# One batch row ahead of the other three: reordering a two-layer decode step so that w_up and w_down are read once

## Chip, cores, metric

The kernel runs on one core of a Trainium2 chip. The time is the device time of one execution in microseconds (us). Executions come in a fast and a slow state; the medians and ratios below are those of fast runs alone. PE is the matmul engine, DVE the vector engine, ACT the scalar engine, and SP the engine whose queue issues the loads. The recorded texts call a row a batch, the gated block glu and layer norm LN. A "tile" here is 1 MiB of the on-chip arena (128 partitions x 4096 bf16), and most loads fill one tile.

## The reference

Two identical layers, with the same weights and the same K and V caches, on four batch rows of one token each. Every layer is a windowed attention and a gated block, each with a residual:

```python
x = x + A(layernorm(x), k_cache, v_cache, wq, wo)   # 32 heads, 8 KV heads, window 2048, head size 128
x = x + B(layernorm(x), w_gate, w_up, w_down)       # sigmoid(x @ w_gate) * (x @ w_up) @ w_down, F = 1792
x = x + A(...)                                      # the same K, V and weights again
x = x + B(...)
```

In bf16 the used part of K is 16 MiB and of V 16 MiB, wq and wo are 4 MiB each, and w_gate, w_up and w_down are 1.75 MiB each. All of it is more than the arena holds (25 tiles), so part of it is read twice.

## The kernel before

It plans all work as operations with tokens that they read and write, orders them per engine with a simple list scheduler, and emits five in-order instruction streams. Loads go out from one queue in a fixed order, and a load can be issued only when a tile of a small pool is free. All 16 K tiles stay in the arena from layer 1 to layer 2; V is read twice (but for two tiles), wq twice, and the gated block's weights twice. A unit of attention is one KV head of all four batch rows: K transposes on DVE (layer 1 only), scores S on PE, softmax on DVE and ACT, a transpose of the probabilities on PE, then PV on PE, then wo.

```python
pool.free = list(range(4 * HKV, NS, 2))        # 9 tiles for all that is not K
# ... load order: what comes next is taken when a tile is free
load_wq(0)
# ... K and V of layer 1 by head, wo
load_glu(0)                                    # w_gate, w_up, w_down
load_wq(1)
# ... V of layer 2 in reverse order of heads, all but two tiles that were kept
load_glu(1)                                    # w_gate, w_up, w_down once more, last of all

def attn(L):                                   # 8 units, one KV head of 4 rows each
    # ...
    for ui, h in enumerate(hs):
        if ui + 2 < HKV:
            ks[ui + 2] = front(ui + 2)         # scores and softmax, two units ahead
        ov = pv_unit(tag, h, ks[ui], v_tiles[(L, h)])          # 2 tiles, 64 matmuls
        if ui + 2 < HKV:
            turn_p("%d.%d" % (L, ui + 2), ks[ui + 2])          # transposed probabilities
        wo_unit(tag, h, ov, ks[ui], ui == 0, ui == HKV - 1)    # 16 matmuls

# the program
q_proj(0, 0, NB)
attn(0)
glu(0, 0, NB)
layer_norm("Q", 0, NB)
q_proj(1, 0, NB)
attn(2)
glu(1, 0, NB, True)
```

## Time and profile before

| | before |
|---|---|
| median (2 runs) | 185.54 us (185.33 to 185.75) |
| span of the profiled run | 184.4 us |
| bytes on the load queue | 71.84 MB |
| mean DMA rate | 391 GB/s |
| busy share of PE, DVE, ACT | 55%, 49%, 19% |

From the page of the kernel before (busy time by engine; tenths of busy time in 40 equal slices; the load queue; the chain of waits that ended last):

```profile
span 184.4 us, 4421 instructions
PE 101.2 (55%) x1944; PEld 54.7 (30%) x1944; DVE 89.5 (49%) x221; ACT 35.7 (19%) x100; POOL 14.8 (8%) x77
...
DMA  5999999999999999999999999999999999999980
GB/s 198 425 427 427 425 403 391 411 421 419 409 387 425 419 421 403 392 419 419 400 391 414 412 407 393 403 350 417 330 396 419 419 423 416 418 416 402 412 341 24
...
q1 hardware_dynamic: 15352, 71.84, 97.2%
...
DMA 52%; PE 25%; SPq 16%; DVE 4%; issue 2%; ACT 0%
```

The DMA row is at 9 everywhere but at the two ends, and no compute engine is busy for 60% of the span. The kernel is bound by its stream of loads. The Trainium skill ("Perfetto Trace Analysis", Roofline) says that a single core is bounded by its 16 DMA engines at about 435 GB/s; this trace reaches 427.

The same by stage: most of layer 1's attention (0 to 83), the rest of it (to 107.4), the boundary between layers (to 129.1, where layer 2's first score matmul starts), layer 2's attention (to 171.5, the end of its last PV), and the tail. The columns are the stretch, its length, busy time with the number of instructions for each engine, granted PE clock, DMA share and GB/s:

```profile
0.00:83.00 83.00, 34.97 (x580) 16.11 (x580) 51.00 (x99) 15.31 (x42) 7.42 (x39) 0.75 1.00 401
83.00:107.40 24.40, 11.56 (x298) 8.76 (x298) 10.22 (x19) 1.91 (x4) 0.98 (x6) 0.50 1.02 407
107.40:129.10 21.70, 10.47 (x148) 4.33 (x148) 8.04 (x28) 2.42 (x10) 0.00 (x0) 0.50 1.01 393
129.10:171.50 42.40, 37.50 (x836) 22.10 (x832) 16.90 (x64) 14.58 (x39) 6.39 (x33) 0.82 1.01 405
171.50:184.40 12.90, 6.70 (x86) 3.36 (x86) 3.38 (x13) 1.52 (x6) 0.00 (x0) 0.74 0.62 248
```

The boundary is a serial chain of 21.7 us (PE busy for 10.5 of it), yet the stream runs through it at 393 GB/s, because there is always something left to read for later. And in layer 2's attention PE is busy for 37.5 of 42.4 us, so it is close behind the stream: eight units in 42.4 us are 5.3 us each (4.7 of them busy), while the two V tiles of a unit take 2 x 2.49 = 4.98 us to land.

### The profile page before, as it was taken

The page shows a single profiled execution, that of the slowest core. Times are in us where ns is not written, and L with a number is a line of the kernel's source. Part 1 is how long each engine was busy: PE and PEld are TensorE (multiplying, and loading weights), DVE is VectorE, ACT ScalarE, POOL GpSimd, SP SyncE. Part 2 cuts the span into 40 slices and gives each one's busy share as a digit, 9 for nine tenths or more (in the row PEclk, how much of TensorE's full clock was granted, in tenths as well). Part 3 has the DMA queues.
Part 4 walks back from the last instruction along what each step waited for, and adds up shares of the span by engine and source line. Part 5 has one row for each costly group of instructions (what it writes and reads, how often), then busy time and mean ns, then how long its engine had stood idle before and what let it go on. Part 6 is the DMA issues. An engine that isn't in the chain of part 4 may idle for free.

```text
span 184.4 us, 4421 instructions
## 1 busy us (share of the span) xinstructions
PE 101.2 (55%) x1944; PEld 54.7 (30%) x1944; DVE 89.5 (49%) x221; ACT 35.7 (19%) x100; POOL 14.8 (8%) x77
## 2 busy tenths in 40 slices
PE   0532423652807327173373545445979997994474
PEld 0101000332303323023232441210334653584422
DVE  5209998477592565925621531138463442340330
ACT  2003022240212103011020001001365442220010
POOL 4000000110000101010010000000022111120000
PEclk9999995585766756755555555555897897885569
DMA  5999999999999999999999999999999999999980
GB/s 198 425 427 427 425 403 391 411 421 419 409 387 425 419 421 403 392 419 419 400 391 414 412 407 393 403 350 417 330 396 419 419 423 416 418 416 402 412 341 24
DMA packets 15379, 72.12 MB, mean 391 GB/s; under 512 B 1144, under 2 KB 5248, under 8 KB 8704
## 3 DMA queue, kind: packets, MB, share of 16 engines
q1 hardware_dynamic: 15352, 71.84, 97.2%
q8 instruction: 15, 0.25, 0.5%
q14 instruction: 4, 0.03, 0.0%
q10 hardware_dynamic: 8, 0.00, 0.0%
HBM read 71.83 MB, written 0.00 MB: 390 GB/s over the span
## 4 chain that ended last, share of the span: by engine, by line
DMA 52%; PE 25%; SPq 16%; DVE 4%; issue 2%; ACT 0%
DMA arena<-in_A_v_cache_dram 33%; SPq L382 16%; PE ps L697 11%; DMA arena<-in_B_w_down_dram 9%; PE ps L770 8%; DMA arena<-in_A_wq_dram 5%; DMA arena<-in_B_w_up_dram 5%; PE ps L726 2%; PE ps L794 1%; DVE ps L492 1%; PE ps L626 1%; DVE nmax L705 1%; PE ps L749 1%; PE ps L905 1%; PE ps L852 1%
## 5 line engine op out<-in xcount | busy, mean ns | idle before, releaser
L770 PE MATMUL ps<-ebuf,arena 128*128 128x8 bf16 x1024 | 31.0, 167 | 29.7 <-DMA arena<-in_A_v_cache_dram 22.1
L697 PE MATMUL ps<-arena,qbd 128*16 128x512 bf16 x256 | 32.5, 626 | 16.9 <-DVE qbd L668 8.4
L770 PEld LDWEIGHTS ps<-ebuf,arena 128*128 128x128 bf16 x1024 | 28.8, 101 | 36.3 <-DMA arena<-in_A_v_cache_dram 32.5
L678 DVE STREAM_TRANSPOSE arena<-arena 128x1024 f32<-128x1024 f32 x32 | 37.9, 1219 | 3.3 <-DMA arena<-in_A_k_cache_dram 3.0
L705 DVE TENSOR_REDUCE nmax<-ps 128x1 f32<-128x512 f32 x16 | 11.0, 687 | 26.0 <-PE ps L697 26.0
L714 ACT ACTIVATE prow<-ps,nmax 128x512 bf16<-128x512 f32 x16 | 11.0, 687 | 39.6 <-DVE nmax L711 24.9
L671 ACT COPY qbd<-qrep 32x64 bf16<-32x64 bf16 x32 | 7.7, 241 | 40.9 <-PE ps L697 40.3
L697 PEld LDWEIGHTS ps<-arena,qbd 128*16 128x16 bf16 x256 | 6.1, 97 | 31.3 <-issue 22.0
L739 POOL CAST s<-psm 128x1 bf16<-128x1 f32 x16 | 3.0, 188 | 144.4 <-ACT prow L714 144.4
L778 DVE TENSOR_TENSOR onb<-ps,rinv 128x16 bf16<-128x16 f32 x16 | 2.9, 184 | 21.1 <-PE ps L770 21.1
L626 PE MATMUL ps<-arena,xn 128*4 128x512 bf16 x64 | 7.8, 582 | 7.6 <-DMA arena<-in_A_wq_dram 6.2
L794 PE MATMUL ps<-onb,arena 128*128 128x4 bf16 x256 | 9.1, 166 | 3.1 <-DVE onb L778 3.1
L731 ACT CAST prow<-ps 128x512 bf16<-128x512 f32 x16 | 9.4, 587 | 7.1 <-PE ps L726 7.0
L735 DVE STREAM_TRANSPOSE ebuf<-prow 128x256 f32<-128x256 f32 x16 | 7.0, 437 | 6.7 <-ACT prow L731 6.4
L852 PE MATMUL ps<-arena,xn 128*4 128x448 bf16 x64 | 6.5, 560 | 4.9 <-DVE xn L607 3.1
L794 PEld LDWEIGHTS ps<-onb,arena 128*128 128x128 bf16 x256 | 7.9, 101 | 4.1 <-DVE onb L778 2.8
L726 PE MATMUL ps<-prow,perm 64*128 64x256 bf16 x64 | 7.4, 315 | 2.4 <-ACT prow L714 2.3
L596 ACT ACTIVATE lnv<-lnv 128x4 f32<-128x4 f32 x4 | 0.8, 205 | 34.0 <-DVE lnv L593 34.0
L634 DVE STREAM_TRANSPOSE ebuf<-ps 128x512 f32<-128x512 f32 x4 | 2.9, 715 | 7.7 <-PE ps L626 7.6
L859 DVE STREAM_TRANSPOSE ebuf<-ps 128x448 f32<-128x448 f32 x4 | 2.6, 650 | 7.8 <-PE ps L852 7.8
L668 DVE COPY qbd<-qrep 32x64 bf16<-32x64 bf16 x32 | 5.3, 166 | 0.7 <-ACT qrep L657 0.2
L749 PE MATMUL ps<-sel_b,s 128*128 128x16 bf16 x48 | 3.8, 175 | 3.2 <-POOL s L743 2.4
(61 smaller groups left out, 68.1 us busy)
## 6 DMA issues: line engine op xcount, KB each, us to landing
arena<-in_A_v_cache_dram SPq DMA_DIRECT2D x30, 1024.0 KB, 16.8
arena<-in_A_k_cache_dram SPq DMA_DIRECT2D x16, 1024.0 KB, 16.0
arena<-in_A_wq_dram SPq DMA_DIRECT2D x8, 1024.0 KB, 9.4
arena<-in_A_wo_dram SPq DMA_DIRECT2D x4, 1024.0 KB, 24.3
arena<-in_B_w_gate_dram SPq DMA_DIRECT2D x4, 896.0 KB, 19.7
arena<-in_B_w_up_dram SPq DMA_DIRECT2D x4, 896.0 KB, 15.8
arena<-in_B_w_down_dram SPq DMA_DIRECT2D x2, 1024.0 KB, 12.5
arena<-in_B_w_down_dram SPq DMA_DIRECT2D x1, 768.0 KB, 7.0
```

What stands on the lines that cost most here:

```text
L382: o = P.op("sync", name, 0.0, lambda e, dst=dst, src=src: e.dma_start(dst, src), r=r, w=w, dma_bytes=nbytes, dma_rate=tm[rate])
L626: last = pe.matmul(ps[32 * hh:32 * hh + NB, qb, :], xn[:, c * NB:(c + 1) * NB], tile_ap(s)[:, o + hh * 512:o + (hh + 1) * 512], start=(c = ...
L671: P.op("scalar", "qe%s_%d" % (tag, a), c_act(64), lambda s_, dst=dst, src=src: s_.copy(dst, src), r=rd, w=[("q", k2, a)])
L678: P.op("vector", "T%d_%d" % (h, t), c_dve(1024), lambda v, v32=v32: v.transpose(v32, v32), r=[("slot", 4 * h + t)], w=[("slot", 4 * h + t)])
L697: last = pe.matmul(ps[32 * gi:32 * gi + NR, bank, :], qbd[:, q0:q0 + NR], kt[:, cp // 2, cp % 2, b % 2, :, :], start=(cp == 0), stop=(cp = ...
L705: lambda v: v.tensor_reduce(nmax[:, k2:k2 + 1], ps[:, bank, :], AXX, ALU.max),
L714: lambda a: a.activation(prow[:, :].rearrange("p (m x t) -> p m x t", x=16, t=2), ps[:, bank, :].rearrange("p (m t x) -> p m x t", x=16, t ...
L726: last = pe.matmul(ps[:, PBS[i], 0:256], perm[64 * i:64 * i + 64, jh * 128:(jh + 1) * 128], prow[64 * i:64 * i + 64, jh * 256:(jh + 1) * 2 ...
L731: lambda a: a.copy(prow[:, :].rearrange("p (y i t) -> p i y t", i=2, t=2), ps[:, PBS[0]:PBS[0] + 2, 0:256].rearrange("p i (y t) -> p i y t ...
L770: last = pe.matmul(ps[:, ob, bp * 8:bp * 8 + 8], src[:, j * 128:(j + 1) * 128], ev[:, j % 2, j % 16 // 2, x0:x0 + 8], start=(j == 0), stop ...
L794: last = pe.matmul(ps[:, WB, c * NB:(c + 1) * NB], tile_ap(s)[:, o + r_ * D + c * 128:o + r_ * D + (c + 1) * 128], ov[:, r_ * NB:(r_ + 1) ...
L852: last = pe.matmul(ps[32 * g:32 * g + NB, OBS[n], 0:NF], xn[:, c * NB:(c + 1) * NB], tile_ap(s)[:, o:o + NF], start=(c == 0), stop=(c == N ...
```

## The change

Batch row 0 runs both layers first, then rows 1 to 3 follow, with row 0's second attention beside their first. A unit of attention becomes four KV heads of one row. The gain is meant to come from bytes: K of row 0 leaves the arena early, so there is room for w_up and w_down to stay in the arena from one layer to the next (wo was read once before too). w_up and w_down are now read once (3.5 MiB saved), and V of row 0 is read once (2 MiB saved on balance, as before kept two V tiles). wq, w_gate and the rest of V are still read twice. The code says 63 MiB in place of 68.5.

```diff
-        pool.free = list(range(4 * HKV, NS, 2))
+        pool.free = list(range(0, NS - 2, 2))          # 24 tiles, K among them
@@ the unit: four heads of one row
-        def pair_d(cache, h, bp):
-            return cache[2 * bp:2 * bp + 2, h, SK - W:SK, :].rearrange("b (p j) d -> p b (j d)", p=64)
+        def pair_d(cache, b, h):
+            return cache[b, h:h + 2, SK - W:SK, :].rearrange("h (p j) d -> p h (j d)", p=64)
@@ ... wo after the units of a group, 64 matmuls for four heads, in place of 16 for one
@@ the loads
+        load_gu("wg", 0, 3 if "wg" in EVICT else 4)     # uses before the tile is free
+        load_gu("wu", 0, 3 if "wu" in EVICT else 4)
+        load_wd()
+        ...                                             # K and V of rows 1 to 3
         load_wq(1)
+        for b, hu in b_units[::-1]:
+            for bp in (1, 0):
+                load_kv("V", b, hu, bp, 1, 1)           # V of rows 1 to 3 again
+        for nm in ("wg", "wu"):
+            if nm in EVICT:                             # EVICT = ("wg",)
+                load_gu(nm, 1, 1)
@@ the program
-        attn(0)
-        glu(0, 0, NB)
-        layer_norm("Q", 0, NB)
-        q_proj(1, 0, NB)
-        attn(2)
-        glu(1, 0, NB, True)
+        run(a1, {a1[0]: [wo_of("A0", 0, 0)], a1[1]: [wo_of("A0", 0, 1)]})
+        add_wo("A0", 0, 1)
+        glu("A0", 0, 1, (0, 0))
+        layer_norm("QA", 0, 1)
+        q_proj("A", 0, 0, 1, PBS)
+        def a2_tail():
+            add_wo("A2", 0, 1)
+            glu("A2", 0, 1, (0, 0))
+        run(a2 + b1, {a2[0]: [wo_of("A2", 0, 0)], a2[1]: [wo_of("A2", 0, 1), a2_tail],
+                      b1[2]: [wo_of("B0", 1, 0)], b1[5]: [wo_of("B0", 1, 1)]})
+        add_wo("B0", 1, NB)
+        glu("B0", 1, NB, (0, 0))
+        layer_norm("QB", 1, NB)
+        q_proj("B", 1, 1, NB, OBS)
+        run(b2, {b2[2]: [wo_of("B2", 1, 1)], b2[5]: [wo_of("B2", 1, 0)]})
+        add_wo("B2", 1, NB)
+        glu("B2", 1, NB, ..., True)
```

(Bank assignments, scratch buffers and scheduler constants are left out.)

## The prediction

> **What bounds it now.** The kernel streams HBM. The 40-slice view shows the DMA row at 9 in every slice but the first and last two, and GB/s at 391-427; the Trainium skill ("Perfetto Trace Analysis", Roofline) puts one core's ceiling near 435 GB/s for its 16 DMA engines, and this trace reaches 427. PE is busy 55%, DVE 49%, ACT 19%. The bytes are 71.84 MB on the load queue (queue table). K and V tiles of 1 MiB land every 2.49 us (starts of matmuls that wait for V: 98.64, 101.14, 103.61), w_gate/w_up tiles every 2.3. After the last load only two groups of down matmuls and the store remain: about 3 us.
>
> **What the change does to bytes.** From the code: before 68.5 MiB; after 4 (wq) + 16 (K) + 4 + 12 + 12 (V) + 4 (wo) + 3.5 + 1.75 (glu) + 4 (wq again) + 1.75 (w_gate again) = 63 MiB, 66.1 MB. Saved: 5.5 MiB x 2.49 us = 13.7 us, if the stream never stops.
>
> **What it costs.** Resident tiles fill the arena: wo 4, w_gate 2, w_up 2, w_down 1, K of batches 1-3 12, of 24 tiles. At the layer boundary of batches 1-3 three tiles stream, five once w_gate goes. Loads then wait for PE. I followed the order with the trace's durations: LN 2.4 us, a 32-matmul PV 1.02, wo of four heads 4 x 0.57, q 4.1, gate+up 3.3, sigmoid chain to hT 1.0, down 1.85, S 2.0, K transpose 1.22 each. A load into an empty queue takes 5.0 us from issue to landing (first wq: 0.80 to 5.8); the skill ("DMA: Bandwidth & Descriptors", fixed plus bytes/436e3) gives an estimate of 4.4.
> 1. Loads run ahead until about 66 us. Batch 0's second q projection frees the first wq tile at about 65: stall about 1.
> 2. 66-125 us: layer 2 of batch 0 and its glu sit in one in-order PE stream ahead of batches 1-3. Six units of K transposes (29 us) plus softmax, q and LN work make about 52 us of DVE in that stretch, nearly as much as the 59 us of loads. Unit 3's PV comes after that glu, so loads behind it wait: stall 2-6.
> 3. The boundary: wo, LN, gate, up, down, LN, q, about 17 us, in which five tiles (12.5 us) can be loaded. Two stalls, at w_gate's release (about 2) and at wq's (about 4).
> 4. Tail: after the last V come PV 1.0, wo 2.3, LN 2.6, gate+up 3.4, chain 1.1, down and copy 2.4, store 1.8: about 15 us, of which w_gate's 4.5 us is loaded under it. Before: 3 us after the last landing. Net loss about 7 us.
>
> Sum: -13.7 + 1 + 4 + 6 + 7 = +4 at worst latencies, near 0 with 4.4 us landings. The saved bytes go to starved loads and a longer tail.
>
> **Predicted: 186 us**, 80% range 181 to 191; faster by over 2%: 0.14, within 2%: 0.64, slower: 0.22.
>
> **What would show it.** Load queue 66.1 MB; the DMA row at 9 until about 65 us, then dips (below 350 GB/s) around 105-125 us and a clear hole of 3 us or more around 135-145; last V lands at about 167-172; afterwards no full DMA for over 8 us. SP waits on PV (L727) and q (L580) matmuls grow.
>
> **What would make it wrong.** If DVE/PE keep ahead of the loads in 66-125 us, step 2 vanishes and the time is about 181. If a starved queue restarts more slowly than 5 us, or PE's order blocks more (S waiting for K transposes in front of PV), it passes 190.

## More of the kernel before

The times at which loads land and instructions are fetched are read from the packed traces; no view prints them.

The end of PE's timeline before (start, duration, engine, line, instruction, count, and the idle time before with what ended it):

```profile
168.41 1.77 PE L770 MATMUL ps<-ebuf,arena 128*128 128x8 bf16 x61 [2.43 <-issue]
...
171.75 0.59 PE L794 MATMUL ps<-onb,arena 128*128 128x4 bf16 x16 [0.29 <-DVE onb L778]
...
175.36 3.05 PE L852 MATMUL ps<-arena,xn 128*4 128x448 bf16 x32 [1.71 <-DVE xn L607]
...
181.17 1.01 PE L905 MATMUL ps<-arena,hT 128*4 128x256 bf16 x12 [0.20 <-DMA arena<-in_B_w_down_dram]
```

The last matmuls, of w_down, wait for their load: the last weights land 2.7 us before the span ends. So before, the end is paced by loads.

## The result, and the profile after

The changed kernel takes 193.17 us (192.97 and 193.37, two runs) against 185.54: it is slower, at a ratio of 1.0407 with a 95% interval of 1.0365 to 1.0449. Ratios here are the mean time of one kernel's fast runs over the mean of the other's fast runs of the same rounds, so not quite the ratio of the medians quoted.

The page of the kernel after, the same lines:

```profile
span 191.2 us, 5473 instructions
PE 119.7 (63%) x2446; PEld 69.8 (36%) x2446; DVE 91.2 (48%) x249; ACT 38.4 (20%) x114; POOL 14.9 (8%) x78
...
DMA  5999999999999789999999698889859999997000
GB/s 195 425 427 428 420 418 401 347 349 390 403 420 422 291 332 425 425 422 420 418 420 416 250 375 329 334 316 402 263 210 386 428 418 430 415 413 298 8 3 1
...
q1 hardware_dynamic: 14088, 66.07, 86.9%
...
PE 34%; SPq 22%; DMA 17%; DVE 16%; issue 6%; ACT 2%; POOL 0%; DVEq 0%; ACTq 0%
```

The bytes fell as computed, from 71.84 to 66.07 MB. But the GB/s row now has holes near 65 us, between 105 and 145 us, and almost nothing in the last three slices (8, 3 and 1 GB/s). In the chain, DMA has gone from 52% to 17%; PE, DVE and the issuing queue that waits for tiles (SPq) have taken its place.

By stage, in the changed kernel: row 0 up to its second layer (0 to 61), row 0's layer 2 and layer 1's attention of rows 1 to 3 (to 127.6), their boundary (to 145.9), their layer-2 attention (to 178.1), the tail:

```profile
0.00:61.00 61.00, 24.59 (x462) 12.87 (x462) 22.39 (x55) 7.19 (x20) 3.81 (x20) 0.74 1.00 388
61.00:127.60 66.60, 48.08 (x1044) 29.41 (x1044) 46.99 (x111) 16.48 (x49) 6.08 (x32) 0.68 0.92 372
127.60:145.90 18.30, 11.59 (x220) 6.46 (x220) 6.34 (x27) 2.81 (x12) 0.14 (x1) 0.59 0.83 301
145.90:178.10 32.20, 27.46 (x602) 16.06 (x591) 12.15 (x45) 10.44 (x27) 4.85 (x25) 0.71 0.94 386
178.10:191.20 13.10, 7.94 (x136) 4.98 (x134) 3.34 (x13) 1.49 (x6) 0.00 (x0) 0.68 0.01 2
```

These two tables give an account of the difference. Take 405 GB/s, what the kernel before moves in its last attention, as a full stream. A stage's lost stream time is its length times (1 - its rate / 405):

| lost stream time, us | before | after |
|---|---|---|
| up to the end of layer 1's attention (before: 107.4 us; after: 127.6 us) | 0.7 | 2.6 + 5.4 |
| boundary | 0.6 | 4.7 |
| last attention | 0.0 | 1.5 |
| tail | 5.0 | 13.0 |
| sum | 6.3 | 27.2 |

The change saves 5.7 MB (72.12 to 66.42 MB in all queues), worth 14.1 us at that rate, and loses 20.9 us of streaming. The difference is +6.8 us, which is the difference of the spans. This is arithmetic: it tells where the stream was idle, not which wait a remedy must go for. The experiments are for that.

What ended PE's idle times in the last attention, 145.9 to 178.1 us (line and what it waited for: us in total, times, longest):

```profile
PE ps L727 <- issue: 4.1, 3, 2.0
PE ps L602 <- DVE qh L593: 1.2, 1, 1.2
PE ps L683 <- ACT prow L671: 0.6, 1, 0.6
```

There is no wait for V (L727 is PV). The stage belongs to PE: six units in 32.2 us are 5.4 us each. And 4.1 us of it is "issue": time in which PE waits for nothing that a semaphore shows. PE's timeline shows the pattern:

```profile
164.18 0.74 PE L727 MATMUL ps<-ebuf,arena 128*128 128x8 bf16 x24 [1.35 <-issue]
164.85 1.96 PE L652 MATMUL ps<-arena,qbd 128*16 128x512 bf16 x16
166.74 0.61 PE L683 MATMUL ps<-prow,perm 64*128 64x256 bf16 x4
167.28 0.25 PE L706 MATMUL ps<-sel_b,s 128*128 128x16 bf16 x3
167.38 1.85 PE L749 MATMUL ps<-on_b,arena 128*128 128x3 bf16 x64
169.09 0.59 PE L727 MATMUL ps<-ebuf,arena 128*128 128x8 bf16 x17
170.41 1.41 PE L727 MATMUL ps<-ebuf,arena 128*128 128x8 bf16 x47 [0.73 <-issue]
...
176.51 1.63 PE L727 MATMUL ps<-ebuf,arena 128*128 128x8 bf16 x55 [2.01 <-issue]
178.42 1.86 PE L749 MATMUL ps<-on_b,arena 128*128 128x3 bf16 x64 [0.28 <-DVE on_b L735]
...
183.00 3.16 PE L785 MATMUL ps<-arena,xn 128*3 128x448 bf16 x32 [1.42 <-DVE xn L562]
...
187.29 1.69 PE L838 MATMUL ps<-arena,hT 128*4 128x256 bf16 x28 [0.54 <-DVE hT L807]
```

Count the matmuls between the first two gaps: 24 + 16 + 4 + 3 + 64 + 17 = 128. Each comes with one weight load (the page counts both alike), so 256 instructions. The Trainium skill ("Runtime: NRT & Kernel Launch", Instruction fetch mechanics) says that an engine's instructions are refilled in blocks of 16 KiB, 256 instructions, over a DMA queue, and that the cost of crossing from one to the next is "mostly hidden".

The trace agrees on the block: it has fetches of 16,384 bytes that begin at 161.62, 167.84 and 174.11 us and take about 1.1 us each, and the three gaps end 1.3 to 1.5 us after those fetches do. Counted over PE's whole stream of matmuls and weight loads, all five "issue" gaps of this trace, both of the trace of before, and all 34 in the traces of the runs below come at the same place modulo 256 (instruction 193 or 194). By count it agrees on "mostly" too (19 fetches on the instruction queue, 5 gaps over 0.4 us), but these five cost PE 7.3 us in all, 4.1 of them here. Before had two such gaps, 3.4 us in all. The longer one ended in the same moment as the last V landed (168.41), but the matmul that waits for that tile started only at 170.46, so PE was held back there too. It did not set the end, which the loads of w_down did: b_pvhalf below has no such gap and is no faster.

The last V lands at 173.61 us and the last PV ends at 178.14: PE finishes its own backlog of 4.5 us. After that there is nothing left to load, and the serial tail takes 13.1 us.

### The profile page after: what moved, and what is told of

Read it like the earlier page. It is cut to its first block, busy times and chain, and to the rows that moved or that the text cites. A ratio compares the mean times of both kernels' runs of the same rounds, so it can differ in the third digit from the quotient of the medians.

```text
span 191.2 us, 5473 instructions
## 1 busy us (share of the span) xinstructions
PE 119.7 (63%) x2446; PEld 69.8 (36%) x2446; DVE 91.2 (48%) x249; ACT 38.4 (20%) x114; POOL 14.9 (8%) x78
## 2 busy tenths in 40 slices
DMA packets 14119, 66.42 MB, mean 347 GB/s; under 512 B 1032, under 2 KB 5136, under 8 KB 7824
## 3 DMA queue, kind: packets, MB, share of 16 engines
q1 hardware_dynamic: 14088, 66.07, 86.9%
## 4 chain that ended last, share of the span: by engine, by line
PE 34%; SPq 22%; DMA 17%; DVE 16%; issue 6%; ACT 2%; POOL 0%; DVEq 0%; ACTq 0%
SPq L377 22%; PE ps L727 9%; DMA arena<-in_B_w_down_dram 8%; PE ps L652 8%; DVE arena L632 7%; DMA arena<-in_A_k_cache_dram 5%; PE ps L749 5%; DMA arena<-in_A_v_cache_dram 3%; PE ps L785 3%; PE ps L683 3%; PE ps L862 2%; PE ps L580 2%; DVE nmax L662 2%; DVE arena L792 2%; PE ps L539 1%
## 5 line engine op out<-in xcount | busy, mean ns | idle before, releaser
L727 PE MATMUL ps<-ebuf,arena 128*128 128x8 bf16 x1024 | 29.6, 167 | 11.2 <-issue 5.0
L727 PEld LDWEIGHTS ps<-ebuf,arena 128*128 128x128 bf16 x1024 | 28.3, 101 | 12.8 <-issue 9.5
L580 PE MATMUL ps<-arena,xn 128*4 128x512 bf16 (+2 forms) x96 | 11.2, 609 | 7.7 <-DVE xn L562 4.7
L785 PE MATMUL ps<-arena,xn 128*1 128x448 bf16 (+1 forms) x128 | 11.5, 511 | 6.8 <-DVE xn L562 4.2
L749 PE MATMUL ps<-on_a,arena 128*128 128x1 bf16 x256 | 8.3, 166 | 10.3 <-DMA arena<-in_A_wo_dram 8.0
L551 ACT ACTIVATE lnv<-lnv 128x1 f32<-128x1 f32 (+2 forms) x7 | 1.4, 204 | 54.7 <-DVE lnv L548 54.7
L749 PEld LDWEIGHTS ps<-on_a,arena 128*128 128x128 bf16 x256 | 7.6, 104 | 11.4 <-DMA arena<-in_A_wo_dram 8.3
L792 DVE STREAM_TRANSPOSE arena<-ps 128x448 f32<-128x448 f32 x8 | 5.1, 639 | 11.2 <-PE ps L785 9.5
L735 DVE TENSOR_TENSOR on_b<-ps,rinv 128x16 bf16<-128x16 f32 x12 | 2.2, 179 | 17.4 <-PE ps L727 17.4
L588 DVE STREAM_TRANSPOSE arena<-ps 128x512 f32<-128x512 f32 x6 | 4.2, 703 | 9.9 <-PE ps L580 9.8
L785 PEld LDWEIGHTS ps<-arena,xn 128*1 128x1 bf16 (+1 forms) x128 | 3.6, 100 | 13.0 <-issue 6.1
```

The lines of the kernel that those rows point to most:

```text
L580: last = pe.matmul(ps[32 * hh:32 * hh + nb, qb, :], xn[:, c * NB + b0:c * NB + b1], tile_ap(s)[:, o + hh * 512:o + (hh + 1) * 512], start= ...
L727: last = pe.matmul(ps[:, ob, bp * 8:bp * 8 + 8], src[:, j * 128:(j + 1) * 128], ev[:, j % 2, j % 16 // 2, x0:x0 + 8], start=(j == 0), stop ...
L749: last = pe.matmul(ps[:, WB, c * nb:(c + 1) * nb], tile_ap(s)[:, o + r_ * D + c * 128:o + r_ * D + (c + 1) * 128], on[:, q0:q0 + nb], star ...
L785: last = pe.matmul(ps[32 * g:32 * g + nb, PBS[n], 0:NF], xn[:, c * NB + b0:c * NB + b1], tile_ap(s)[:, o:o + NF], start=(c == 0), stop=(c ...
L792: lambda v, n=n: v.transpose(gbuf[:, 0:NF], ps[:, PBS[n], 0:NF].rearrange("p (x k) -> p k x", k=NFC)),
```

## The experiments

Theory at this point: three things took the saved 14 us. **S** (stream): row 0's second gated block sits in the in-order PE stream in front of PV of rows 1 to 3, which holds tiles and starves the loads in the middle. **P** (PE): in the last attention PE, with its instruction waits (**I**), is the limit, and not the loads. **T** (tail): the bytes saved were loaded under serial chains before, so they were worth little. Rival **L**: the kernel is still bound by its loads to the last V; stalls of the stream, at the boundary above all, are the loss, and PE follows. Rival **Q** to I: the instruction fetches suffer from the number of loads queued ahead of them.

Eleven kernels ran in three calls; the kernel before ran beside each, with medians of 185.85, 185.71 and 185.7 us. The changed kernel was not run again: its 193.17 us and its ratio are from the first comparison, beside 185.54 us. The ratios are the safer measure.

| label | what | median, us | ratio to before, 95% interval |
|---|---|---|---|
| (after) | the change | 193.17 | 1.0407 [1.0365, 1.0449] |
| a_v2half | after, half of layer 2's V not loaded | 189.00 | 1.0154 [1.0095, 1.0213] |
| a_pvhalf | after, half of layer 2's PV matmuls | 189.55 | 1.0154 [1.0073, 1.0234] |
| a_v2half_pvhalf | after, both | 183.45 | 0.9895 [0.9848, 0.9941] |
| a_merge_wo_glu | after, row 0's second wo and gated block done with the others' | 188.32 | 1.0099 [1.0043, 1.0155] |
| a_merge_glu | after, only its gated block | 188.54 | 1.0160 [1.0123, 1.0197] |
| m_v2half | a_merge_wo_glu and a_v2half | 184.44 | 0.9937 [0.9898, 0.9976] |
| a_evict2 | after, two more tiles free at the boundary | 193.09 | 1.0422 [1.0343, 1.0501] |
| a_sems3 | after, at most 3 loads in flight | 191.35 | 1.0302 [1.0215, 1.0390] |
| m_sems3 | a_merge_wo_glu and a_sems3 | 191.72 | 1.0323 [1.0239, 1.0406] |
| b_glu1_sliver | before, 4.5 MiB less to load at the end | 185.06 | 0.9921 [0.9861, 0.9980] |
| b_pvhalf | before, half of layer 2's PV matmuls | 186.31 | 1.0039 [0.9981, 1.0098] |

All were fast runs but for the profiled run and one more of a_v2half_pvhalf, the profiled run of a_sems3 and one run of before, which are left out of the medians and ratios.

### a_v2half: are loads the limit of the last attention?

Layer 2's V tiles of rows 1 to 3 are loaded by half, 6 MiB less; the planner is told the full size, so that the order stays. The other half of a tile holds old data, so the kernel computes something else, though within the tolerance of the comparison.

```diff
-            load((kind, b, hu, bp, k), n_use, "bw_8k",
-                 (2 * SLOT, pair_d(A_k if kind == "K" else A_v, b, hu * 4 + 2 * bp), True))
+            src = pair_d(A_k if kind == "K" else A_v, b, hu * 4 + 2 * bp)
+            n = SLOT if k == 1 else 2 * SLOT
+            load((kind, b, hu, bp, k), n_use, "bw_8k", (n, src[:, :, 2 * SLOT - n:2 * SLOT], True), 128 * 4 * SLOT)
```

> The changed kernel, but each of the twelve V tiles that layer 2 of batches 1-3 reads again is loaded by half (0.5 MiB instead of 1 MiB, 6 MiB less in all; result wrong on purpose). Order of instructions unchanged. Theory P (in the last attention PE sets the end: 32.2 us from the first score matmul to the last PV, then 13 us of serial tail): 191 to 193.2 us, against 193.2 for the changed kernel. Rival L (the end is set by the loads, whose last V tile lands at 173.6): the last V lands 8 to 12 us earlier and the time falls by 3 us or more, below 190. Sub-theory I (the three idle times of PE in this stage, 4.1 us, are PE's instruction blocks waiting behind the data in the DMA engines): these gaps shrink to under 2 us, and the time falls by about as much.

The last V landed at 160.88 us, 12.7 us earlier than after the change. The time fell by 4.2 us only. PE's waits in its last attention (146.0 to 174.4 us):

```profile
PE ps L603 <- ACT qbd L625: 1.2, 1, 1.2
PE ps L684 <- ACT prow L672: 0.6, 1, 0.6
PE ps L728 <- issue: 0.4, 1, 0.4
```

Compare with the same lines after: the two small waits are the same, and "issue" has gone from 4.1 to 0.4 us. The stage took 28.25 us in place of 32.2. So what halving the loads gave is about what the instruction waits had cost; 12.7 us of earlier V gave nothing beyond. The time alone does not decide: P without I (191 to 193.2) missed, and 189.0 lies where L had put it (below 190). The trace does: PE waits for no V here, before or after the cut. L falls for this stage and P with I stands: without the waits for instructions PE needs 28 us here, however early V comes.

### a_pvhalf: is PE?

```diff
-                    for j in range(2 * NJ):
+                    nj = NJ if tag[0] == "2" and b > 0 else 2 * NJ
+                    for j in range(nj):
```

(The last matmul's stop flag goes with it. The output is wrong.)

> The changed kernel, but the PV matmuls of layer 2 of batches 1-3 are halved (16 of 32 per tile; result wrong on purpose), all loads kept. That takes about 12 x 0.45 = 5 us from PE in the last attention. Theory P: PE no longer lags, the loads set the end (last V at about 173.6, PV right after it), so the time falls by 3 to 4 us, to 189-190. Rival L: the end follows the last V tile as before, 192.5 to 193.2.

It gave 3.6 us, and PE's backlog became a wait for V:

```profile
PE ps L728 <- DMA arena<-in_A_v_cache_dram: 4.6, 3, 1.9
```

The last V landed at 174.55 us and the last PV ended 0.6 us later. So PE was the limit, and the loads are close behind it: with PE relieved, they are the next limit within 4 us. The "issue" waits of this stage are gone here too, so this run can't tell PE's matmuls from its instruction waits. The next one can.

### a_v2half_pvhalf: both

The two edits together.

> Changed kernel with both reliefs of the last attention: its V tiles of batches 1-3 loaded by half (6 MiB less) and its PV matmuls of batches 1-3 halved. Wrong result on purpose. One relief alone gave 189.0 (loads) and 189.6 (PE). If loads and PE each bound that stage within about 4 us of each other (my theory now), both together give much more than either: last PV ends near 168-170, time 183 to 186. If instead the instruction fetches alone were what either relief removed, there is nothing left to take and the time stays at 188 to 189.

183.45 us, 9.7 less than after the change, where each alone gave about 4. Had each edit only removed the instruction waits, nothing would have been left to gain. This is what two limits close to each other look like: relieving one leaves the other.

### a_merge_wo_glu and a_merge_glu: row 0's second gated block out of the way

Row 0's second wo and gated block join the final ones of rows 1 to 3, at four columns in place of three. Both kernels compute the right result.

```diff
         def a2_tail():
             add_wo("A2", 0, 1)
-            glu("A2", 0, 1, (0, 0))
...
-        glu("B2", 1, NB, tuple(1 if nm in EVICT else 0 for nm in ("wg", "wu")), True)
+        glu("B2", 0, NB, tuple(1 if nm in EVICT else 0 for nm in ("wg", "wu")), True)
```

(This is a_merge_glu, with the use counts of the tiles adapted; a_merge_wo_glu moves the wo matmuls as well.)

> The changed kernel, but the wo and the glu of batch 0's layer 2 are not done beside the first attention of batches 1-3; they join those of batches 1-3 at the end (four columns instead of three). Result correct. PE loses 128 + 88 matmuls between 83 and 107 us, DVE about 2 us of small work, and the loads wait less for PV in front of them. Theory S (batch 0's second wo and glu, in one in-order stream with the first attention of batches 1-3, are what holds back PV there and so the loads: the last V tile of layer 1 lands at 126.5): it lands 3 to 5 us earlier, time 188 to 190. Rival D (the K transposes on DVE set the pace there): it lands within 1.5 us of before, time 191.5 to 193.

> Changed kernel with only batch 0's second gate/up/down block merged into the final one (wo not merged). Correct result. Both merged gave 188.3, that is 4.9 us less than the changed kernel. If the gate/up/down block in the in-order PE stream is what holds the PV behind it (prediction's step 2), this alone gives most of it: 188 to 190, last layer-1 V at 122 to 124 us. If the 2.3 us of wo matmuls do as much, it gives half: 190.5 to 191.5.

188.32 and 188.54 us: 4.9 and 4.6 less than after the change. The last layer-1 V landed at 122.13 us in both, against 126.50, so rival D falls. The gated block alone does it; the 128 wo matmuls are worth at most about 1 us (the ratios differ by 0.6%, and their intervals overlap). The stages of a_merge_glu, cut at the same events as after (the last layer-1 PV, layer 2's first scores, its last PV; its first 61 us are the same):

```profile
61.00:124.50 63.50, 44.95 (x954) 26.53 (x954) 44.88 (x99) 15.63 (x44) 6.12 (x32) 0.69 0.97 393
124.50:143.20 18.70, 11.94 (x223) 6.58 (x221) 6.44 (x27) 2.82 (x12) 0.00 (x0) 0.53 0.85 286
143.20:173.40 30.20, 27.03 (x586) 15.78 (x586) 11.97 (x44) 10.45 (x27) 4.91 (x25) 0.82 0.99 407
173.40:186.90 13.50, 8.34 (x135) 5.02 (x134) 3.38 (x13) 1.52 (x6) 0.00 (x0) 0.65 0.02 7
```

The middle took 63.5 us in place of 66.6, with the stream at 393 GB/s in place of 372: 3.1 us. Theory S holds: in the changed kernel this block stands between PV and the tiles that PV frees. Its own wait there is on DVE: PE waits 2.7 us, up to 105.73 us, for the transpose of gate or up, which DVE takes in turn with K transposes of 1.2 us each. The boundary is as long as after, and the last attention is 2.0 us shorter: with a different place of the block ends in PE's stream, its "issue" waits were 2.5 us in place of 4.1. That second part was not expected.

### m_v2half: do the two gains add?

> Changed kernel with batch 0's second wo and gate/up/down merged into the final ones, and the V tiles of the second layer of batches 1-3 loaded by half. If the two gains are in different stages (stream in the middle 4.9 us, instruction waits and V at the end 4.2 us), they add: 193.2 - 4.9 - 4.2 = 184 (183 to 185.5). If both relieve the same thing, it stays at 187 to 188.5.

184.44 us: they do. The sum was 184.1. The losses in the middle and in the last attention are separate, and neither hides the other. The end of PE's timeline there:

```profile
163.15 1.80 PE L728 MATMUL ps<-ebuf,arena 128*128 128x8 bf16 x64
164.87 0.61 PE L684 MATMUL ps<-prow,perm 64*128 64x256 bf16 x4
165.41 0.25 PE L707 MATMUL ps<-sel_b,s 128*128 128x16 bf16 x3
165.51 3.55 PE L728 MATMUL ps<-ebuf,arena 128*128 128x8 bf16 x128
169.36 1.87 PE L750 MATMUL ps<-on_b,arena 128*128 128x4 bf16 x64 [0.29 <-DVE on_b L736]
```

V has long landed (157.80 us), no "issue" gap is left in this attention, and still the span is 182.2 us: from the last PV at 169.06 the serial tail takes 13.1 us. This kernel loads 11.5 MiB less than before, and is 0.6% faster (and computes something else).

### a_evict2: the boundary's stalls

```diff
-    EVICT = cfg.get("EVICT", ("wg",))
+    EVICT = cfg.get("EVICT", ("wg", "wu"))
```

w_up is given up at the boundary too and read again at the end: two more tiles for V, 1.75 MiB more to read.

> The changed kernel, but w_up is given up after the glu of batches 1-3 as w_gate is, and read again at the end: two more free tiles at the layer boundary, 1.75 MiB more to read. Result correct. The prediction's step 3 took the stalls of the stream at the boundary (about 6 us) for lost time. If the stream there sets the time (theory L), the V loads of layer 2 start about 7 us earlier and the time falls by 2 us or more. Theory P (PE sets the end from the boundary on): the last V lands some us earlier, the end does not move: 192 to 194 us. The idle times of PE for instructions (4.1 us) stay, for the data stream now runs on to the end of the attention.

The last V landed at 170.16 us in its profiled run, 3.4 us earlier than after, and the median is 193.09 us against 193.17. A gain of 1 us can't be excluded (the interval's low end is 0.6% under the changed kernel's ratio, and the profiled run was the fastest of four, at 191.88), but one of 3.4 us can. PE was the limit behind it again: its last PV ended 6.6 us after the last V landed (4.5 after the change), with 3.7 us of "issue". So the stalls of loads at the boundary are real and lie off the critical path.

### a_sems3 and m_sems3: is it the depth of the queue?

The number of completion semaphores, 24, becomes 3, which allows three loads in flight at most. If instruction fetches wait behind queued loads, they should get shorter.

> The changed kernel with 3 DMA semaphores instead of 24, so that at most three loads are in flight (7.5 us of backlog instead of up to 20); nothing else. If PE's instruction blocks queue behind the backlog of data (theory Q), the idle times of PE marked issue in the last attention (4.1 us) fall below 2 us, and the time by about as much: 190 to 191.5. If they only share the engines with whatever data moves at the moment (theory B), they stay within 1 us of 4.1 and the time within 1 us of 193.2 (or is a little longer, by thin restarts).

> The version with batch 0's second wo and glu merged into the last ones (188.3 us), with 3 DMA semaphores. Theory Q: its 3.2 us of idle PE for instructions in the last attention shrink to under 1.5, time 186 to 187. Theory B: 188 to 189.

a_sems3 took 191.35 us, 1.8 less than after, with intervals that overlap. That lies in Q's range (190 to 191.5), but its one profile is of a slow run (4.3 us of instruction waits in the last attention), so it can't say why, and this run decides nothing. m_sems3 took 191.72 us, 3.4 us more than a_merge_wo_glu, outside what either theory said. In its profile, of a fast run, the instruction waits of the last attention are 2.5 us, where a_merge_wo_glu has 3.2 and Q had asked for under 1.5. And one of 3.0 us came in the tail's wo matmuls, where a_merge_wo_glu has none; that is most of the 3.4 us:

```profile
173.46 1.07 PE L749 MATMUL ps<-on_b,arena 128*128 128x4 bf16 x34 [0.29 <-DVE on_b L735]
177.53 0.94 PE L749 MATMUL ps<-on_b,arena 128*128 128x4 bf16 x30 [3.00 <-issue]
```

Rival Q is not borne out: with three loads in flight at most the waits did not go away. The fetch before that gap began at 175.29 us, when PE had been idle for 0.8 us, and took 0.93 us, no longer than others. So the wait here is for the fetch to begin, and then 1.3 us from its end to the next matmul.

What decides when it begins stays open, but the traces hold a lead. Take the place in PE's stream where the gaps come as the crossing into a new block. In the traces of after, a_v2half, m_v2half and m_sems3, eight such crossings have no load in flight, and the next fetch begins 0.4 to 1.1 us later. Before the three last gaps of after it began 4.3, 3.7 and 3.7 us after the preceding crossing, and before the three of m_sems3 3.2, 3.7 and 4.8 us, with at most three loads in flight. At other crossings with loads in flight it is anything from 0.4 to 5.2 us, so this is no proof.

What the runs show of I is where the waits are: while loads are in flight (4.1 us after, 2.5 and 3.2 in the merged kernels, 3.0 in the tail of m_sems3, whose loads ended at 175.90), and hardly where V had come by half (0.4 us and none). With PV halved there were none either, though all loads ran: there PE waits for V. No run changed the fetches alone.

### b_glu1_sliver: what were the bytes at the end of before worth?

Before, with the second read of w_gate, w_up and w_down cut to slivers, 4.5 MiB less, the planner told the full size. Its output is wrong, which doesn't matter for the time.

```diff
+                    if k == 1:
+                        load((nm, cc, k), 2, "bw_3k", (F // 4, src[:, 2 * cc, 0:F // 4], False), 128 * 4 * F)
+                    else:
                         load((nm, cc, k), 2, "bw_3k", (2 * F, src[:, 2 * cc:2 * cc + 2, :], False))
```

(And the same for w_down.)

> The kernel before, but of the second reading of gate, up and down only a sliver is loaded (0.8 of 5.25 MiB; result wrong on purpose); nothing else changes. That removes about 4.5 MiB, 11 us of the stream at 2.49 us per MiB. If bytes are time, as the prediction's first term says: about 175 us. If a late load is worth only what lies behind it after the last PV (theory W): the last attention ends at 171.5 as before, LN, gate, up, chain, down and store take about 11 us, so 182.5 to 184.5.

The loads ended at 170.29 us, 11.5 us earlier than before, and the time fell by 0.8 us. Its timeline at the end:

```profile
167.52 1.77 PE L776 MATMUL ps<-ebuf,arena 128*128 128x8 bf16 x61 [1.92 <-issue]
...
170.86 0.59 PE L800 MATMUL ps<-onb,arena 128*128 128x4 bf16 x16 [0.29 <-DVE onb L784]
...
174.47 3.16 PE L858 MATMUL ps<-arena,xn 128*4 128x448 bf16 x32 [1.71 <-DVE xn L613]
...
178.86 2.04 PE L911 MATMUL ps<-arena,hT 128*4 128x256 bf16 x28 [0.39 <-DVE hT L880]
```

Compare 168.41, 171.75, 175.36 and 181.17 before. Everything up to gate and up moves by 0.9 us. Theory T holds: before, the second read of the gated block's weights was loaded under a chain that takes its time anyway. Of the 5.5 MiB that the change saves, 3.5 are of this kind.

### b_pvhalf: does before have PE's limit too?

The edit of a_pvhalf in the kernel before, for all of layer 2.

> The kernel before with half of the PV matmuls in layer 2 (as a_pvhalf does for the changed kernel; result wrong on purpose), all loads kept: about 7 us of PE less between 130 and 171. In the kernel before the loads go on to 181.75 and the last down tiles are waited for, so: 184.8 to 185.8 us, within 0.5% of before, where the same cut took 3.6 us off the changed kernel. If PE sets the end there too: 180 or less.

186.31 us, no gain. There loads pace the end (the last of w_down landed at 181.72), so the PE limit of the last attention is the changed kernel's own.

No right version beats the kernel before: the best, a_merge_wo_glu, is 1% slower.

## Why the prediction was wrong, point by point

| step | predicted | measured |
|---|---|---|
| bytes | 66.1 MB | 66.07 MB |
| 1. stall at wq's release | about 1 us at about 65 | 1.2 us: the load that lands at 71.02 comes 3.65 after the one before it, where 2.49 is usual |
| 1 and 2. stalls up to 125 us | 3 to 7 us | 5.4 us of lost stream in 61 to 127.6 us |
| 3. boundary | two stalls, 6 us | 4.7 us of lost stream, and 1.5 in the attention after it |
| 4. last V lands | 167 to 172 us | 173.61 us |
| 4. from there to the end | about 15 us | 17.6 us |

(Its reading of the GB/s row before, 391 to 427, leaves out three slices of 387, 350 and 330; nothing rests on it.)

**Right:** the bytes; that the stream would starve, where and why (a_merge_glu shows the gated block in front of PV); that the tail would be bare; the direction of the larger risk. The prediction's sum at worst latencies, +4 us, would be 189.5 us.

**The step that failed** is 4, "after the last V come PV 1.0, wo 2.3, LN 2.6, ...". It takes it that PE has followed the loads up to the last V, and only one PV of 1.0 us is left. The runs show that PE is the limit of the last attention: from the last V's landing to the end of the last PV it took 4.5 us, not 1.0, because six units need 32.2 us, of which 4.1 us are waits for instructions. The term of the sum is 3.5 us short. By size the instruction waits, for which the sum has no term, are what is missing: without them the last PV would end at about 174.0 us (an estimate, 178.1 less 4.1), 0.4 us after the last V, and a_v2half, with 0.4 us of them, took 28.25 us for the stage. The rest of the tail was sized well: 13.1 us against 13.6 from the prediction's own durations. The trace of before had what was needed: 5.3 us on PE for a unit in the last attention (4.7 busy, 0.4 of waits for instructions) against 4.98 of loads, 88% of busy PE there, and two gaps marked "issue". In a kernel that is bound by loads they cost nothing, and the prediction did not ask what they would cost once loads thin out.

**The second error** is the middle of the sum. It ran from +4 us with restarts of 5.0 us, which the trace of before showed, to 0 with 4.4 us, an estimate from the Trainium skill ("DMA: Bandwidth & Descriptors", Anatomy of one DMA: about 2.0 us fixed plus bytes over 436 GB/s). The page states this fit for loads that gpsimd issues; here the sync engine issues them, and the prediction does not say so. It settled near the lower end. Measured in an empty queue, the first load of wq took 4.94 us before and 4.89 after. The restarts of the changed kernel took 4.70, 4.89 and 4.94 us (landings at 71.02, 113.57, 146.81); the queue was not quite empty then, as one load was still in flight and landed 1.0 to 1.1 us after the issue. The trace's own number should have been used, and it would have given 189.5. Adding the missing 3.5 gives 193.0, close to the 193.17 measured. That closeness is partly luck: step 3 was counted as time, and a_evict2 shows that these stalls are off the path, because PE's backlog grows by what the loads gain.

**Where the gain went:** the 14.1 us that the saved bytes are worth in a full stream were a price that the kernel before did not pay in full. Its second read of the gated block's weights was nearly free (b_glu1_sliver: 4.5 MiB for 0.8 us). In their place came a starved middle (a_merge_glu shows 3.1 us there, of its 4.6) and a last attention at PE's pace (about 4 us for either relief, 9.7 for both). What stays open is why the instruction fetches begin late, and what the serial boundary (18.3 us) and tail (13.1 us) would give if they were shorter: no run shortened those chains alone.

## What to carry to other kernels

Before you count saved bytes as time, ask of each byte what ran beside its load: a read under a serial chain is nearly free, and taking it away leaves the chain. Size the runner-up in every stage, gaps included (here PE at 5.3 us a unit, 4.7 of them busy, against loads at 5.0), since the first limit hides it. The Trainium skill ("Perfetto Trace Analysis", Optimization Strategy) says that the most-contended engine can change over time within a kernel; here it did, and in the last attention the two limits lay within 4 us of each other. Work that goes early into an in-order engine stream holds back whatever frees tiles behind it, so postpone what nobody waits for: moving row 0's last gated block to the end was worth 4.6 us, 3 of them in the stage where it had stood.

## What the Trainium skill lacked or had wrong

- "Runtime: NRT & Kernel Launch", Instruction fetch mechanics: crossing a 16 KiB block is called mostly hidden. Here five crossings of 19 fetched blocks cost PE 0.7 to 2.3 us each, 7.3 us of a 191 us span; in the last attention the waits went from 4.1 to 0.4 us when half as much V was loaded, and did not go away with at most 3 loads in flight (2.5 us there and 3.0 in the tail, in m_sems3). The page gives no figure for the whole of such a wait: the fetches before these gaps took 0.9 to 1.1 us, and PE went on 1.2 to 1.6 us after their ends.
- "DMA: Bandwidth & Descriptors", Anatomy of one DMA: its fit is stated for the gpsimd path, and the page has none for loads that the sync engine issues. Taken over to them, it gives an estimate of 4.4 us for 1 MiB; issued into an empty queue such loads took 4.94 and 4.89 us here.
